# Two PSUM banks for the scores of the row maxima and two for the transposed scores and the turned maxima, instead of one pool of four

## The chip, the cores and the metric

The kernel runs on one core of a Trainium2 chip, and its time is device microseconds of one execution. The core has five engines that run side by side and meet through semaphores: TensorE (PE; its weight loads are listed apart, as PEld), VectorE (DVE), ScalarE (ACT), GpSimd (POOL) and SyncE (SP), which here issues transfers alone. PE writes its results into PSUM, which has eight banks of 128 partitions x 512 float32. PE works at a granted clock of 1.2 or 2.4 GHz, which the profile lists as 0.5 or 1.0.

## The reference

There are 8 batches of 8 heads, 576 positions and 64 columns. Each head is a causal attention with a decay bias that comes from running sums of `s`; the batch's rows, all heads side by side, then go through a selection of 128 of the 576 rows and a two-layer network for those rows alone.

```python
scores = scale * np.matmul(q, k.transpose(0, 1, 3, 2))
cum = np.cumsum(np.maximum(s, 0.0), axis=-1)
bias = -(cum[:, :, :, None] - cum[:, :, None, :])
scores = np.where(causal, -1000000000.0, scores + np.minimum(bias, 0.0))
scores = scores - np.max(scores, axis=-1, keepdims=True)
attn = np.exp(scores)
attn = attn / (np.sum(attn, axis=-1, keepdims=True) + 1e-09)
out = np.matmul(attn, v)
...
top_idx = np.argpartition(-(x @ w_gate)[b], capacity)[:capacity]
xe = x[b, top_idx]
ye = np.maximum(xe @ w1, 0.0) @ w2
out[b, top_idx] = xe + sigmoid(xe @ w_gate)[:, None] * ye
```

## The kernel before

**One head.** The 64 heads (8 batches x 8) are a stream through the same steps, and several heads are under way at a time. The scores of a head are computed twice. First with queries on the partitions, for the row maxima alone (`s_part`, line 335, in four parts): part 0 holds the query blocks 1 and 2 (192 and 320 columns), part 1 the blocks 3 and 0 (448 and 64), parts 2 and 3 the block 4 (512 and 64). Each part is one PSUM tile named `s`; DVE reads it with the mask and leaves the maximum (`s_max`, `mj<-s,maskf` in the profile; the result is `m`, of part 2 `md`). Then `m_rows` (line 372) has PE turn the 128 x 5 maxima into 5 x 128, ACT copies them out (`mr`), and a transfer lays them as a row into `qa`. With that row as one more line of the contraction, `st_part` (line 392) computes the transposed scores with their maxima subtracted, in higher precision by a second matmul into the same bank (`st<-qa,ka`, then `st<-qb,kb`); its parts 0 to 3 begin with 448, 320, 288 and 288 columns. ACT takes the exponential of each part (`pt<-st`), POOL clears the masked corner, and `av` multiplies by the values (`pa<-vt,pt`); DVE normalizes into `xt`.

**The batch's choice and network.** After a batch, `choose` scores the rows on DVE, turns the scores on PE in two tiles (`sct`, copied out by ACT as `row`), compares on DVE (`ahead`, `hit`), and sums positions on PE (`pidx`). `expert` does the network for two batches together, in small steps (`ph`, `py`) between the heads' steps. The last two batches' networks come after the last head.

**What sets the order.** Every engine runs its instructions in program order. A written list, `START`, gives the steps of the first heads, mixed with matmuls that only keep PE busy (`fill`, tile `warm`); after it a table, `SCHEDULE`, places each step of head n at slot 8n plus an offset. In the steady stretch PE's order in a head is: part 0 of `s` (head n+2), the last of `av`, part 1 of `s`, the turn of the maxima of head n+1, parts 0 and 1 of `st` (head n), three `av` products, part 2 of `s`, three more, part 3 of `s`, parts 2 and 3 of `st`, four more.

**The banks.** The pool `psS` (line 127) has four banks under one tag, `s`. Parts of `s`, parts of `st`, `sct` and `pidx` take whichever is free; the turned maxima are put into the last 128 columns of the bank of part 3 of `s` (kept as `st[n]["tp"]`, line 370), so that this bank is held until ACT has copied them out. After the last head, the tiles of the network take banks of this pool too (`bank`, line 589). `psA` has two banks for `pa`, `psM` two for the network, the warm matmuls and a few more.

Of the kernel before, what the change touches and what calls it, by code (L numbers as in the profile page):

```python
# [7 lines left out]
F32 = mybir.dt.float32  # L8
# [5 lines left out]
ALU = mybir.AluOpType  # L14
AX = mybir.AxisListType
PSUM = bass.MemoryType.PSUM
# [3 lines left out]
def _f(ap):  # L20
    return ap.bitcast(F32)
# [45 lines left out]
def kernel(  # L67
# [12 lines left out]
    pe, dve, act, pool, sp = (  # L80
        InOrder(tc, e) for e in (nc.tensor, nc.vector, nc.scalar, nc.gpsimd, nc.sync)
    )
    P = 128
# [4 lines left out]
    NT = (S + P - 1) // P  # L88
    LAST = S - (NT - 1) * P
    PAD = P - LAST  # L90
    SP = S + PAD
# [32 lines left out]
    small = ctx.enter_context(tc.tile_pool(name="small", bufs=3))  # L124
    moe = ctx.enter_context(tc.tile_pool(name="moe", bufs=1))
    dram = ctx.enter_context(tc.tile_pool(name="dram", bufs=2, space=bass.MemoryType.DRAM))
    psS = ctx.enter_context(tc.tile_pool(name="psS", bufs=4, space=PSUM))
    psA = ctx.enter_context(tc.tile_pool(name="psA", bufs=1, space=PSUM))
    psM = ctx.enter_context(tc.tile_pool(name="psM", bufs=2, space=PSUM))

# [149 lines left out]
    vts, xts, st = {}, {}, {}  # L280
# [46 lines left out]
    def s_max(n, u, scores, init=2.0 * NEG, c0=None, out=None):  # L327
        w = scores.shape[1]
        junk = small.tile([P, 512], BF16, tag="mj", name=f"mj{n}_{u}", bufs=2)
        dve.tensor_tensor_reduce(  # L330
            junk[:, 0:w], scores, maskf[:, S - w : S] if c0 is None else maskf[:, c0 : c0 + w], 1.0, init,
            ALU.add, ALU.max, out[:, 0:1] if out is not None else st[n]["m"][:, u : u + 1],
        )

    def s_part(n, part):
        i = n % NB
        ka, qa = KA[i], QA[i]
        if part == 0:
            st[n]["m"] = small.tile([P, NT], F32, tag="m", name=f"m{n}")
            st[n]["md"] = small.tile([P, 1], F32, tag="md", name=f"md{n}")  # L340
        R = RS
        tp = psS.tile([P, 512], F32, tag="s", name=f"s{n}_{part}")

        def mm(u, o_ap, c0):
            w = o_ap.shape[1]
            pe.matmul(
                o_ap, qa[0:R, u * P : (u + 1) * P], ka[0:R, c0 : c0 + w], start=True, stop=True
            )

        W = [LAST + u * P for u in range(NT)]  # L350
        if part == 0:
            a1, a2 = tp[:, 0 : W[1]], tp[:, W[1] : W[1] + W[2]]
            mm(1, a1, 0)
            mm(2, a2, 0)
            s_max(n, 1, a1)
            s_max(n, 2, a2)
        elif part == 1:
            a3, a0 = tp[:, 0 : W[3]], tp[:, W[3] : W[3] + W[0]]
            mm(3, a3, 0)
            mm(0, a0, 0)  # L360
            s_max(n, 3, a3)
            s_max(n, 0, a0)
        elif part == 2:
            mm(4, tp, 0)
            s_max(n, 4, tp, c0=0, out=st[n]["md"])
        else:
            a4 = tp[:, 0 : S - 512]
            mm(4, a4, 512)
            s_max(n, 4, a4, st[n]["md"][:, 0:1])
            st[n]["tp"] = tp  # L370

    def m_rows(n):

        i = n % NB
        m = st[n]["m"]
        row = QA[i][RM[i] : RM[i] + 1]
        tp = st[n]["tp"]
        if n == 0:
            tpm = psM.tile([P, 512], F32, tag="misc", name="tpm0")
            for t in range(NT):  # L380
                o_ap = tpm[0:1, t * P : (t + 1) * P] if t < 4 else tp[0:1, 512 - P : 512]
                pe.transpose(o_ap, m[:, t : t + 1], ident)
            act.activation(row[:, 0:512], tpm[0:1, :], AF.Copy, scale=-1.0)
            dve.tensor_scalar(row[:, 512:SP], tp[0:1, 512 - P : 512], -1.0, None, op0=ALU.mult)
            return
        tpm = tp[0:NT, 512 - P : 512]
        pe.transpose(tpm, m, ident)
        mr = small.tile([NT, P], F32R, tag="mr", name=f"mr{n}")
        act.activation(mr, tpm, AF.Copy, scale=-1.0)
        act.dma_start(_f(row).rearrange("a (t c) -> a t c", c=P), _f(mr))  # L390

    def st_part(n, part):
        i = n % NB
        R = RM[i] + 1
        ka, kb, qa, qb = ka_all[:, i, :], kb_all[:, i, :], QA[i], QB[i]
        if part == 0:
            st[n]["pt"] = ptp.tile([P, PTW], F32, tag="pt", name=f"pt{n}")
        pt = st[n]["pt"]
        tp = psS.tile([P, 512], F32, tag="s", name=f"st{n}_{part}")
        plan = [  # L400
            [(1, 0, cols[1])],
            [(2, 0, cols[2]), (3, 0, cols[3])],
            [(0, 0, HALF)],
            [(0, HALF, HALF), (4, 0, cols[4])],
        ][part]
        o = 0
        for t, c0, w in plan:
            kr = KR[t]
            ks = slice(t * P, t * P + kr)
            qs = slice(PAD + QB0[t] + c0, PAD + QB0[t] + c0 + w)  # L410
            pe.matmul(tp[0:kr, o : o + w], ka[0:R, ks], qa[0:R, qs], start=True, stop=False)
            pe.matmul(tp[0:kr, o : o + w], kb[:, ks], qb[:, qs], start=False, stop=True)
            o += w
        p0 = off[plan[0][0]] + plan[0][1]
        if part == 3:
            act.activation(pt[:, p0 : p0 + HALF], tp[:, 0:HALF], AF.Exp, scale=SCALE)
            act.activation(pt[0:R1, p0 + HALF : p0 + o], tp[0:R1, HALF:o], AF.Exp, scale=SCALE)
        else:
            act.activation(pt[:, p0 : p0 + o], tp[:, 0:o], AF.Exp, scale=SCALE)
        for t, c0, _ in plan:  # L420
            if c0 == 0:
                w = KR[t]
                pool.affine_select(
                    out=pt[0:w, off[t] : off[t] + w], in_=pt[0:w, off[t] : off[t] + w],
                    pattern=[[1, w]], compare_op=ALU.is_ge, fill=0.0, base=QB0[t] - t * P,
                    channel_multiplier=-1,
                )
# [158 lines left out]

    gs = {}

    def bank(shape, name):

        if finishing:
            return psS.tile(shape, F32, tag="s", name=name)
        return psM.tile(shape, F32, tag="misc", name=name)

    def expert(items):
# [5 lines left out]
        for j, (b, si, n, idx, xe) in enumerate(items):  # L601
            tpx = bank([P, NDT, P], f"xt{b}_{si}")
            for c in range(NDT):
                pe.transpose(tpx[:, c, 0:n], xe[0:n, c * P : (c + 1) * P], ident[0:n, 0:n])
            parts = [xh[:, :, P : 2 * P] if single else xl[:, :, j * P : (j + 1) * P]]
            parts.append(xh[:, :, j * P : (j + 1) * P])
            lo, hi = (x[:, :, 0:n] for x in parts)
            act.activation(hi, tpx[:, :, 0:n], AF.Copy)
            dve.tensor_tensor(lo, tpx[:, :, 0:n], _f(hi), op=ALU.subtract)
            if n < P:  # L610
                for x in parts:
                    dve.memset(_f(x[:, :, n:P]), 0.0)
            yield 1
            if not single:
                yield 1
# [3 lines left out]
        if single:  # L619
# [3 lines left out]
            def turn(f0):  # L623
                pt = bank([P, 4, P], name=f"pt{key}_{f0}")
                for f in range(f0, f0 + 4):
                    pe.transpose(pt[:, f - f0, :], hr[:, f * P : (f + 1) * P], ident)
                act.activation(hh[:, f0 : f0 + 4, 0:P], pt, AF.Copy)
                dve.tensor_tensor(
                    hl[:, f0 : f0 + 4, 0:P], pt, _f(hh[:, f0 : f0 + 4, 0:P]), op=ALU.subtract
                )  # L630

            turned = 0
            for f0 in range(0, F, 512):
                ph = bank([P, 512], name=f"ph{key}_{f0}")
                for a, (x0, wi) in enumerate(trip):
                    for c in range(NDT):
                        pe.matmul(
                            ph, xh[:, c, x0 : x0 + P], w1hl[:, wi, c, f0 : f0 + 512],
                            start=(a == 0 and c == 0), stop=(a == len(trip) - 1 and c == NDT - 1),
                        )  # L640
                    yield 1
                    if finishing and a == 0 and turned < f0 // P:
                        turn(turned)
                        turned += 4
                        yield 1
                act.activation(hr[:, f0 : f0 + 512], ph, AF.Relu)
# [85 lines left out]
    def run(op, n):  # L732
# [19 lines left out]
    AVU = [[0, 1], [2], [3], [4]]  # L752
    STAGES = dict(
        load=load, rows=rows, khi=khi, klo=klo, qhi=qhi, kb=kb, qb=qb, qlo=qlo, s=s_part, mrows=m_rows, st=st_part,
        av=lambda n, part: av(n, AVU[part]), norm=norm,
    )
# [10 lines left out]
    for slot_ in range(first, 8 * NH - 7 + max(pos for _, pos in SCHEDULE)):  # L767
        if slot_ >= 0 and slot_ % 2 and slot_ // 8 < len(CFG["fill"]):
            keep_warm(CFG["fill"][slot_ // 8])
        for op, pos in SCHEDULE:  # L770
# [3 lines left out]
            elif (slot_ - pos) % 8 == 0 and 0 <= (slot_ - pos) // 8 < NH:  # L774
                n = (slot_ - pos) // 8
# [57 lines left out]
```

## Time and profile before

| | |
|---|---|
| median of 3 runs | 522.47 us (521.87 to 522.79) |
| profiled execution, its own time | 521.27 us |
| its span (first to last instruction) | 519.6 us |
| PE busy / weight loads busy | 487.6 us / 447.5 us |
| DVE / ACT / POOL busy | 401.9 / 302.8 / 332.5 us |
| mean granted clock of PE | 0.982 |

A row of busy time counts an engine's instructions; of PE the ends are modelled, so that a short stop between two matmuls can hide in the row of the first. A row of waits names the engine that waited, the tile it was about to write and whose instruction ended the wait. A row of a timeline gives the start from the span's begin, the duration, the engine, the operation with its tiles and shapes, how many such instructions follow each other, and in brackets the engine's idle time before it and what ended that. L34 is the line of a helper that all instructions go through, so that the tiles' names tell the steps apart.

### The profile page before, as it was taken

To read this page: it belongs to the slowest core of one execution; us is meant where nothing else is said; L and a number is where in the kernel's file an instruction comes from. 1 tells how busy PE (TensorE), PEld (TensorE's weight loads), DVE (VectorE), ACT (ScalarE), POOL (GpSimd) and SP (SyncE) were. 2 spreads that over 40 slices of the span, in tenths; PEclk is the share of its full clock that TensorE was granted. 3 is DMA by queue.
4 is the path that set the end of the run, shared out by engine and by line. 5 is a ranking of instruction groups with operands and counts; after the bars stand their busy time and mean duration, and the time that the engine had idled before them with its cause. 6 is when DMAs were issued, how large, how long until landed. Compare 5 with 4: busy or idle time off the path is not lost.

```text
span 519.6 us, 11361 instructions
## 1 busy us (share of the span) xinstructions
PE 487.6 (94%) x3845; PEld 447.5 (86%) x3847; DVE 401.9 (77%) x1416; ACT 302.8 (58%) x658; POOL 332.5 (64%) x495
## 2 busy tenths in 40 slices
PE   6999998899988999899999999999999999999995
PEld 2688997889877889799999998999988898999774
DVE  7767898997689898977778986875689887763642
ACT  5566776667566767655555675654576665632121
POOL 6677777778678787865556774654778774523230
PEclk8899998999799999999999999999999999999999
DMA  4234542234324443322123332033242431011210
GB/s 165 79 103 117 183 142 75 89 100 142 105 78 154 135 119 114 118 93 80 41 93 120 113 119 73 2 119 112 73 141 65 143 107 40 8 46 42 67 40 21
DMA packets 23899, 49.08 MB, mean 94 GB/s; under 512 B 2537, under 2 KB 12068, under 8 KB 23842
## 3 DMA queue, kind: packets, MB, share of 16 engines
q1 hardware_dynamic: 19376, 39.52, 24.4%
q10 hardware_dynamic: 3186, 4.65, 2.9%
q0 software_dynamic: 1280, 4.20, 2.3%
q8 instruction: 30, 0.49, 0.4%
q14 instruction: 27, 0.22, 0.1%
HBM read 36.37 MB, written 11.53 MB: 92 GB/s over the span
## 4 chain that ended last, share of the span: by engine, by line
PE 58%; DVE 27%; issue 8%; DMA 3%; ACT 2%; POOL 1%; ACTq 0%; POOLq 0%; SPq 0%; DVEq 0%
PE pa L34 22%; PE st L34 14%; DVE mj L34 10%; PE s L34 7%; PE py L34 6%; DVE ahead L34 4%; DVE qb L34 3%; DVE junk L34 3%; PE warm L34 2%; DVE xt L34 1%; DMA out_dram<-xt 1%; DVE z L34 1%; ACT pt L34 1%; PE sct L34 1%; POOL hit L34 1%
## 5 line engine op out<-in xcount | busy, mean ns | idle before, releaser
L34 PE MATMUL pa<-vt,pt 128*96 128x95 f32 (+2 forms) x1920 | 227.4, 260 | 0.0
L34 PEld LDWEIGHTS pa<-vt,pt 128*96 128x96 f32 (+2 forms) x1920 | 214.7, 177 | 3.7 <-POOL pt L34 0.4
L34 ACT ACTIVATE pt<-st 128x288 f32<-128x288 f32 (+3 forms) x320 | 128.4, 439 | 105.2 <-PE st L34 88.5
L34 POOL TENSOR_SCALAR_AFFINE_SELECT pt<-pt 128x128 f32<-128x128 f32 (+1 forms) x320 | 108.1, 356 | 107.4 <-ACT pt L34 99.4
L34 DVE CUSTOM_DVE_ANT_0 mj<-s,maskf 128x192 bf16<-128x192 f32 (+4 forms) x320 | 139.8, 467 | 46.8 <-PE s L34 46.1
L34 PE MATMUL st<-qa,ka 67*128 67x288 f32 (+9 forms) x384 | 120.9, 326 | 19.1 <-DVE m L34 17.0
L34 PE MATMUL s<-ka,qa 66*128 66x64 f32 (+4 forms) x384 | 109.1, 342 | 3.6 <-DVE ka L34 3.6
L34 POOL TENSOR_TENSOR qb<-qk,qb 64x576 fp32r<-64x576 f32 x62 | 92.6, 1494 | 23.9 <-DVE qb L34 15.0
L34 PE MATMUL st<-qb,kb 128*128 128x288 f32 (+4 forms) x384 | 102.0, 302 | 0.0
L34 POOL TENSOR_TENSOR kb<-qk,ka 64x576 fp32r<-64x576 f32 x64 | 94.4, 1474 | 9.0 <-ACT ka L34 3.6
L34 PEld LDWEIGHTS st<-qa,ka 67*128 67x128 f32 (+3 forms) x384 | 71.9, 187 | 32.5 <-DVE m L34 27.1
L34 PEld LDWEIGHTS st<-qb,kb 128*128 128x128 f32 (+1 forms) x384 | 72.3, 188 | 0.8
L34 PEld LDWEIGHTS s<-ka,qa 66*128 66x128 f32 x384 | 65.5, 195 | 6.5 <-POOL kb L34 4.1
L34 ACT ACTIVATE kb<-qk 64x576 fp32r<-64x576 f32 x64 | 43.6, 682 | 5.5 <-DVE m L34 1.4
L34 ACT ACTIVATE qa<-qk 64x576 fp32r<-64x576 f32 x64 | 43.7, 683 | 4.9 <-DMA qa<-mr 1.5
L34 DVE CAST qb<-qk 64x576 fp32r<-64x576 f32 x64 | 44.8, 701 | 2.0
L34 ACT ACTIVATE ka<-qk 64x576 fp32r<-64x576 f32 x64 | 42.9, 670 | 3.7 <-DVE m L34 3.1
L34 DVE CUSTOM_DVE_ANT_0 junk<-xt,wg 128x512 bf16<-128x512 f32 (+1 forms) x40 | 34.9, 892 | 0.4
L34 ACT ACTIVATE mr<-s 5x128 fp32r<-5x128 f32 x63 | 16.5, 262 | 30.9 <-PE s L34 30.7
L34 DVE TENSOR_TENSOR xt<-pa,z 128x320 f32<-128x320 f32 x64 | 31.2, 487 | 0.1
L34 DVE SCALAR_TENSOR_TENSOR ahead<-row,sc,later 128x576 bf16<-128x576 f32 (+4 forms) x35 | 30.7, 878 | 0.6
L34 POOL DMA_INDIRECT out_dram<-xe,idx x8 | 8.8, 1104 | 33.5 <-DVE xe L34 23.5
(285 smaller groups left out, 536.6 us busy)
## 6 DMA issues: line engine op xcount, KB each, us to landing
qk<-in_qk_dram SPq DMA_DIRECT2D x31, 576.0 KB
vt<-in_v_dram SPq DMA_DIRECT2D x32, 325.0 KB
out_dram<-xt SPq DMA_DIRECT2D x16, 384.0 KB
wr<-in_w_dram ACTq DMA_DIRECT2D x16, 256.0 KB
out_dram<-xt SPq DMA_DIRECT2D x16, 192.0 KB
ka<-cumhl ACTq DMA_DIRECT2D x63, 4.5 KB
qa<-mr ACTq DMA_DIRECT2D x63, 2.5 KB
qk<-in_qk_dram SPq DMA_DIRECT2D x2, 288.0 KB
```

Of the source, the lines that this page charges most:

```text
L34: return self._tc.keep_in_program_order(call(*args, **kwargs))
```

## The change

The pool keeps four banks, now as two tags of two: `s` for the parts of the scores of the maxima (and for `sct` and `pidx`), `t` for the parts of the transposed scores and for the turned maxima, which get a tile of their own, `tpm`, at the turn. So the bank of part 3 of `s` is no longer held for the turn. After the last head the network's tiles take a bank of each tag by turns.

```diff
-    psS = ctx.enter_context(tc.tile_pool(name="psS", bufs=4, space=PSUM))
+    psS = ctx.enter_context(tc.tile_pool(name="psS", bufs=2, space=PSUM))
...
-            st[n]["tp"] = tp
...
-        tp = st[n]["tp"]
+
+        tp = psS.tile([P, 512], F32, tag="t", name=f"tpm{n}")
...
-                o_ap = tpm[0:1, t * P : (t + 1) * P] if t < 4 else tp[0:1, 512 - P : 512]
+                o_ap = tpm[0:1, t * P : (t + 1) * P] if t < 4 else tp[0:1, 0:P]
...
-        tpm = tp[0:NT, 512 - P : 512]
+        tpm = tp[0:NT, 0:P]
...
-        tp = psS.tile([P, 512], F32, tag="s", name=f"st{n}_{part}")
+        tp = psS.tile([P, 512], F32, tag="t", name=f"st{n}_{part}")
...
+    turns = [0]
+
     def bank(shape, name):
 
         if finishing:
-            return psS.tile(shape, F32, tag="s", name=name)
+            turns[0] += 1
+            return psS.tile(shape, F32, tag="st"[turns[0] % 2], name=name)
         return psM.tile(shape, F32, tag="misc", name=name)
```

The instructions of every engine stand in the same order as before; what moves is for whom an instruction waits. On PE in the steady stretch, before, from part 1 of `s` of head 18 (`s18_1`) over the turn of head 17 to the first two parts of `st` of head 16 (in brackets the semaphores that an instruction waits for, by the engine that raises them):

```order
L34 MATMUL s18_1_1726<-ka_89,qa_91 128x448 [waits Activation_49]
L34 MATMUL s18_1_1726<-ka_89,qa_91 128x64
L34 MATMUL s17_3_1683<-ident_116,m17_1626 5x128 [waits DVE_49]
L34 MATMUL st16_0_1739<-qa_91,ka_89 128x448 [waits DMAHW6_49,Activation_49]
L34 MATMUL st16_0_1739<-qb_92,kb_90 128x448
L34 MATMUL st16_1_1744<-qa_91,ka_89 128x320 [waits DVE_49]
```

The same place on PE with the change:

```order
L34 MATMUL s18_1_1743<-ka_89,qa_91 128x448 [waits DVE_49]
L34 MATMUL s18_1_1743<-ka_89,qa_91 128x64
L34 MATMUL tpm17_1750<-ident_116,m17_1642 5x128 [waits Activation_49]
L34 MATMUL st16_0_1757<-qa_91,ka_89 128x448 [waits DMAHW6_49,Activation_49]
L34 MATMUL st16_0_1757<-qb_92,kb_90 128x448
L34 MATMUL st16_1_1762<-qa_91,ka_89 128x320 [waits Activation_49]
```

Part 1 of `st` waited for DVE (in this head for the maxima of part 0 of `s` of head 18, whose bank it takes); it now waits for ACT, which copies the turned maxima out of the bank that it takes. Part 1 of `s` now waits for DVE's maximum of part 3 of the head before.

On PE in `START`, before, around the turn of head 0 and parts 2 and 3 of `s` of head 1:

```order
L34 MATMUL tpm0_230<-ident_116,m0_162 1x128 x3
L34 MATMUL s0_3_188<-ident_116,m0_162 1x128 [waits DVE_49]
L34 MATMUL s1_2_238<-ka_89,qa_91 128x512
L34 MATMUL s1_3_242<-ka_89,qa_91 128x64 [waits DVE_49]
L34 LDWEIGHTS warm_93
```

The same place on PE with the change:

```order
L34 MATMUL tpm0_231<-ident_116,m0_162 1x128 x3
L34 MATMUL tpm0_230<-ident_116,m0_162 1x128
L34 MATMUL s1_2_239<-ka_89,qa_91 128x512 [waits DVE_49]
L34 MATMUL s1_3_243<-ka_89,qa_91 128x64 [waits DVE_49]
L34 LDWEIGHTS warm_93
```

Part 2 took a free bank and now takes that of part 0 of the same head, after DVE's two maxima of it; part 3 took the bank of part 0 and now takes that of part 1, whose maxima DVE computes later.

Where a batch's choice falls between part 2 and part 3 of `s` (once a batch, here head 28), the tile `sct` takes one of the two `s` banks, and part 3 takes the bank of part 2. On PE with the change:

```order
L34 MATMUL s28_2_2720<-ka_89,qa_91 128x512 [waits DVE_49]
...
L34 MATMUL sct2_0_2730<-ident_116,sc2_2609 128x128 x2
L34 MATMUL s28_3_2735<-ka_89,qa_91 128x64 [waits DVE_49]
...
L34 MATMUL sct2_3_2795<-ident_116,sc2_2609 128x96 [waits DVE_49]
```

Before, part 3 there took a bank that ACT had read, and so did the second `sct`; now part 3 waits for DVE's maximum of part 2 just before it, and the second `sct` for DVE's maxima of part 0 of head 29.

## Rows read from the trace of the kernel before

**Rows 1.** The page's first part: busy us, share of the span, instructions.

```profile
PE 487.6 (94%) x3845; PEld 447.5 (86%) x3847; DVE 401.9 (77%) x1416; ACT 302.8 (58%) x658; POOL 332.5 (64%) x495
```

**Rows 2.** The waits of PE and of its weight loads, of two answers: who waited for whom, us in total, times, longest us.

```profile
PE st L34 <- DVE m L34: 17.0, 22, 1.7
...
PE st L34 <- DVE md L34: 1.2, 4, 0.5
...
PEld st L34 <- DVE m L34: 27.1, 27, 2.0
...
PEld st L34 <- DVE md L34: 2.9, 9, 0.7
```

**Rows 3.** Groups of instructions with shapes kept apart, PE: the first matmul of part 1 of `st`; busy us, mean ns, then idle before and what ended it.

```profile
L34 PE MATMUL st<-qa,ka 67*128 67x320 f32 x48 | 17.0, 355 | 14.3 <-DVE m L34 14.2
```

**Rows 4.** Windows, each from the first matmul of part 0 of `st` of one head to that of the next: length, then busy us of PE, PEld, DVE, ACT, POOL, the granted clock, the share of the DMA engines and GB/s.

```profile
101.60:108.31 6.71, 5.82 (x53) 5.39 (x51) 6.61 (x25) 4.30 (x9) 5.29 (x7) 1.00 0.63 180
120.88:126.39 5.51, 5.51 (x52) 5.42 (x51) 3.76 (x17) 4.18 (x9) 4.88 (x10) 1.00 0.04 13
132.20:142.81 10.61, 9.46 (x56) 8.96 (x55) 6.13 (x27) 4.79 (x10) 6.32 (x8) 0.68 0.23 70
378.26:385.55 7.29, 6.27 (x57) 5.83 (x56) 6.50 (x27) 4.68 (x10) 6.65 (x10) 1.00 0.19 74
```

**Rows 5.** Windows over several heads, the same columns.

```profile
95.40:115.40 20.00, 17.84 (x156) 16.46 (x154) 19.65 (x77) 12.81 (x27) 15.10 (x22) 1.00 0.26 78
...
148.70:171.60 22.90, 18.77 (x156) 16.67 (x154) 22.54 (x79) 14.06 (x30) 19.41 (x27) 1.00 0.36 111
...
202.00:217.10 15.10, 12.87 (x110) 11.67 (x108) 14.90 (x52) 10.23 (x22) 13.21 (x18) 1.00 0.34 102
...
285.10:292.30 7.20, 6.23 (x58) 5.71 (x55) 7.07 (x29) 4.29 (x9) 5.34 (x9) 1.00 0.10 37
...
391.10:411.00 19.90, 17.83 (x156) 16.43 (x154) 19.57 (x77) 12.79 (x27) 15.43 (x23) 1.00 0.25 78
```

**Rows 6.** Timeline of the head at 101.6: DVE's second maximum of part 0 of `s`, the first matmul of part 1 of `st`, and part 2 of `s`.

```profile
102.59 0.48 DVE L34 CUSTOM_DVE_ANT_0 mj<-s,maskf 128x320 bf16<-128x320 f32 x1
...
103.14 0.41 PE L34 MATMUL st<-qa,ka 67*128 67x320 f32 x1 [0.89 <-DVE m L34]
...
104.36 0.48 PE L34 MATMUL s<-ka,qa 66*128 66x512 f32 x1
```

**Rows 7.** Timelines around the turn of the maxima, of a head in which nothing waits (at 120.9: the turn, ACT's copy, the weight load and first matmul of part 1 of `st`) and of one in which ACT is late (at 73.9: the same matmul and copy).

```profile
120.85 0.27 PE L34 MATMUL s<-ident,m 128*5 128x128 f32 x1
...
121.16 0.27 ACT L34 ACTIVATE mr<-s 5x128 fp32r<-5x128 f32 x1 [0.40 <-PE s L34]
121.17 0.19 PEld L34 LDWEIGHTS st<-qa,ka 97*128 97x128 f32 x1
121.37 0.31 PE L34 MATMUL st<-qa,ka 97*128 97x320 f32 x1
...
74.44 0.31 PE L34 MATMUL st<-qa,ka 67*128 67x320 f32 x1
75.07 0.25 ACT L34 ACTIVATE mr<-s 5x128 fp32r<-5x128 f32 x1
```

**Rows 8.** Timelines where a batch's choice takes a bank (at 193: DVE's maximum of part 2 of `s`, then part 3; at 439.7: DVE's second maximum of part 0, then the second `sct`), and of part 1 of `s` at 131.6 with DVE's maximum of part 3 of the head before.

```profile
192.68 0.69 DVE L34 CUSTOM_DVE_ANT_0 mj<-s,maskf 128x512 bf16<-128x512 f32 x1
...
193.26 0.28 PE L34 MATMUL s<-ka,qa 66*128 66x64 f32 x1
...
439.72 0.49 DVE L34 CUSTOM_DVE_ANT_0 mj<-s,maskf 128x320 bf16<-128x320 f32 x1
439.73 0.33 PE L34 MATMUL sct<-ident,sc 96*128 96x96 f32 x2
...
131.58 0.48 PE L34 MATMUL s<-ka,qa 66*128 66x448 f32 x2
131.76 0.27 DVE L34 CUSTOM_DVE_ANT_0 mj<-s,maskf,md 128x64 bf16<-128x64 f32 x1
```

**Rows 9.** Timelines of `START`: DVE's second maximum of part 0 of head 0, then part 2 of head 0; part 2 and 3 of head 1 with DVE's last maximum of part 1 of that head; DVE's second maximum of part 0 of head 3 with parts 0 to 2 of head 3 (five matmuls).

```profile
11.15 0.49 DVE L34 CUSTOM_DVE_ANT_0 mj<-s,maskf 128x320 bf16<-128x320 f32 x1
11.21 1.04 PE L34 MATMUL s<-ka,qa 66*128 66x512 f32 x2
16.75 0.63 PE L34 MATMUL s<-ka,qa 66*128 66x512 f32 x2
18.10 0.22 DVE L34 CUSTOM_DVE_ANT_0 mj<-s,maskf 128x64 bf16<-128x64 f32 x1
27.40 1.05 PE L34 MATMUL s<-ka,qa 66*128 66x192 f32 x5
28.22 0.49 DVE L34 CUSTOM_DVE_ANT_0 mj<-s,maskf 128x320 bf16<-128x320 f32 x1
```

**Rows 10.** Windows around the stretches of low clock, columns as in Rows 4.

```profile
15.70:19.10 3.40, 3.40 (x21) 2.20 (x21) 2.72 (x11) 1.27 (x2) 1.43 (x2) 1.00 0.01 3
80.50:83.90 3.40, 1.74 (x14) 1.64 (x14) 3.37 (x15) 1.54 (x4) 3.01 (x5) 1.00 0.09 35
131.70:135.10 3.40, 2.20 (x16) 1.62 (x15) 3.30 (x18) 1.22 (x4) 2.63 (x4) 1.00 0.28 112
135.10:138.50 3.40, 3.40 (x17) 3.30 (x17) 1.95 (x8) 1.47 (x3) 2.23 (x3) 0.50 0.57 161
```

More of the change, by code (lines that the diff above doesn't have):

```diff
@@ L380, in m_rows @@
             for t in range(NT):
-                o_ap = tpm[0:1, t * P : (t + 1) * P] if t < 4 else tp[0:1, 512 - P : 512]
+                o_ap = tpm[0:1, t * P : (t + 1) * P] if t < 4 else tp[0:1, 0:P]
                 pe.transpose(o_ap, m[:, t : t + 1], ident)
             act.activation(row[:, 0:512], tpm[0:1, :], AF.Copy, scale=-1.0)
-            dve.tensor_scalar(row[:, 512:SP], tp[0:1, 512 - P : 512], -1.0, None, op0=ALU.mult)
+            dve.tensor_scalar(row[:, 512:SP], tp[0:1, 0:P], -1.0, None, op0=ALU.mult)
             return
-        tpm = tp[0:NT, 512 - P : 512]
+        tpm = tp[0:NT, 0:P]
         pe.transpose(tpm, m, ident)
```

## The prediction

> **What bounds the kernel now.** I read the page's busy times first: PE 487.6 of 519.6 us, DVE 401.9, ACT 302.8, POOL 332.5 [rows 1]. PE is nearly full, so time can come only from its stops, from loads that are not hidden, and from its clock. Then the waits of PE: the tiles `st` waited for DVE's maxima, 17.0 us in 22 waits and 1.2 us in 4; the weight loads waited 27.1 in 27 and 2.9 in 9 [rows 2]. By groups, 14.3 us of that stand before one matmul, the first of part 1 of `st` [rows 3]. A timeline shows why: DVE's maximum of 320 columns ends at 103.07, the matmul starts at 103.14 after 0.89 idle [rows 6]; it needed a bank whose reader had nothing to do with it. Last the windows of single heads: one with such a stop takes 6.71 us, one without 5.51 [rows 4]. The difference, 1.20, is 0.31 more than the idle shown (0.89), since the next weight load cannot run ahead of a stopped PE; I count 0.3 for each stop.
>
> **What is removed.** Idle 18.2 (17.0 + 1.2) in 26 waits, 26 x 0.3 = 7.8 for loads, and 10 waits that only loads show (36 - 26) x 0.3 = 3.0: 29.0 us gross. Not all of it pays. In five stretches, 85.1 us long in all, PE is busy 73.54 and DVE 83.73 [rows 5]: DVE is the engine that is full. PE idles 11.56 there, some 15 waits at the mean of 18.2 / 26 = 0.70; with 15 x 0.3 they hold 16.0 of the 29.0. What such a stretch can give is DVE's idle, 1.37, at the low end; at the high end one stop more at the edge of each, 5 x 1.20 + 1.4 = 7.4, if PE runs ahead before it and catches up behind it. I take 1.8, near the row of DVE's idle. Outside, 13.0 remain. In two heads with a choice (193 and its twin at 382) part 3 of `s` now takes the bank of part 2, whose maximum ends at 193.37, and the matmul stood at 193.26 [rows 8]: there the wait only moves, minus 2 x 1.20. So 10.6 + 1.8 = 12.4 us are gained.
>
> **What is added at part 1 of `st`.** It now takes the bank of the turned maxima, which ACT copies out. In a head where nothing waited the copy ends at 121.43 and the matmul started at 121.37, its load at 121.17 [rows 7]. With 0.05 for the release the matmul starts at 121.48, 0.11 later, and its load, hidden so far, shows for some 0.10: 0.22 a head. Behind the waiting matmul stand the rest of `st` and three products of `av`, all of PE's queue. 64 - 27 heads did not wait there for DVE [rows 2]; 13 of them have steps of the network or choice between the turn and this part, as I count them in the trace; 24 x 0.22 = 5.3. If all 37 paid it were 8.1, if only the 0.11 shows in 24, 2.6; I keep 5.3. In one head ACT is late, copy ending at 75.32 against a matmul at 74.44 [rows 7]: 0.9.
>
> **What is added at `s`.** In the steady stretch part 0 and part 2 of `s` now wait for DVE's maxima of each other, parts 1 and 3 for the others' of theirs. Part 2 starts at 104.36, the maximum it needs ended at 103.07 [rows 6]: over a microsecond of cover; the other parts have as much outside the full stretches. With a choice it is less. The second `sct` stood at 439.73, DVE's maximum ends at 440.21: 0.54, in two batches 1.1. One part 1 stood at 131.58, its maximum ends at 132.03 [rows 8]: 0.4 with some of it behind an earlier stop. Together 1.5. `sct` is read by ACT, with its row copies before all this, so nothing else is held. Behind the last head the network's tiles alternate between the tags; each product there is read by an engine soon after, and the last `exp` lies before them: about nothing, 0 to 0.5.
>
> **START.** Part 2 of head 0 started at 11.21 and must now wait for the maximum that ends at 11.64: 0.4 to 0.5. Part 2 and part 3 of head 1 stand at 16.75 to 17.38; part 3 takes the bank whose last reader ends at 18.32 [rows 9]; PE has nothing else there, 0.7 to 1.0. Parts 2 and 3 of `st` of head 0 come behind two exponentials, 0.4. Part 2 of head 3 starts with the fourth of five matmuls from 27.40 on (about 27.97) and the maximum ends at 28.71: 0.8. After fills that are hidden otherwise I add 3.0 (1.5 to 4).
>
> **Sum without the clock.** Costs 5.3 + 0.9 + 1.5 + 3.0 = 10.7, gain 12.4: minus 1.7.
>
> A sentence of the Trainium skill speaks against rings of two ("Perfetto Trace Analysis", section Optimizing Tensor Performance, Matmuls): independent groups of matmuls should rotate through different banks, so that the eviction of one overlaps the matmuls of the next. Rows 6 agree in that a bank's reader set PE's start, but the reader there was of another stream; by the rule fewer banks for each stream would cost, by the rows the coupling did.
>
> **The clock.** The granted clock falls behind a stop: in 131.7 to 135.1 PE is busy 2.20 of 3.4 us at 1.00, in 135.1 to 138.5 it is full at 0.50 [rows 10]. The head in which that happens takes 10.61 us at a mean of 0.68, the same kind of head at 378.26 takes 7.29 at 1.00 [rows 4]: 3.3. The stop of 80.5 to 83.9 (PE 1.74 of 3.4) has a like stretch behind it, mostly beside a full DVE (3.37 of 3.4) [rows 10]. I take it that the change shortens the wait ahead of the longer stretch enough that the clock stays up: minus 3.2. Against it, PE in START, full now from 15.7 to 19.1 [rows 10], gets about 1 us of idle.
>
> The skill's page "TensorE: Matmul & The Clock Gate" (section A second HAM failure mode: psum-queue depth-cycling) says that PE which stops briefly again and again while it cycles through few banks gets a clock that goes up and down; by it the short new stops at part 1 would cost clock in every head, which no row here shows, as all waits of rows 2 left the mean clock high.
>
> **Forecast.** 521.27 - 1.7 - 3.2 = 516.4 on the profiled execution's scale; the median lies 1.2 above it, so 517.5 us.
>
> **The rivals.**
> - The clock stays as it is, or its drop moves elsewhere, and the rest nets to minus 1.7 or a little less: 520.8. For it: the choice's heads have less slack after the change than before [rows 8]; against it: the waits ahead of the drop are among those removed.
> - Slower: two banks for `s` are too few. PE, no longer stopped at part 1 of `st`, stops at part 1 of `s` for DVE's last maximum of the head before, as the head at 131.6 would [rows 8]. Then the 10.6 outside the full stretches pay half, 5.3, and the full ones 1.4: 6.7 against 10.7, plus 4.0, with the low clock as before: 525.3, or 526.5 by the median. It decides once the freed waits pay under 9.7, a microsecond less than the costs. For it: DVE is full in 85 us [rows 5]. Against it: cover of over 1 us at part 2 [rows 6].
> - More: the full stretches give 7.4 in place of 1.8, and the turn's wait costs 0.11 in place of 0.22 in each of 24 heads, as its load may be issued before: 5.6 + 2.6 = 8.2 more, 508.2, by the median 509.4. For it: DVE's lead is used up at the heads between stretches; against it: DVE idles so little there.
> - The clock follows the new stops: START falls to 0.50 for a stretch (1.7 for 3.4 us) and the others stay: about 522.5 by the median, no change.
> - That it doesn't do what it says: the bank's wait goes by the names of the tiles; part 1 of `st` can then not wait for `m`. I give it nothing.
>
> **Chances.** Forecast 0.40 (514.5 to 519.5), first rival 0.22, slower 0.18, more 0.14, clock in START 0.06. Half of the first rival's and most of the last fall within 0.2% of the median (1.04 us), which is about what a measurement of this kernel tells from no change. Faster: 0.40 + 0.14 + 0.11 = 0.65; same 0.15; slower 0.20. The range reaches from inside the larger gain to the slower rival, 511 to 526; the likeliest case alone is 514.5 to 519.5.
>
> **What would show it.** Right: `st` no longer waits for DVE's `m` but for ACT's `mr`, by some 0.1 at a time; the stops left stand at `s` in the DVE-full stretches, and the sum of PE's idle falls by several microseconds; DVE's busy time is unchanged; the head at 132 runs at 1.00 in under 8 us. START is 2 to 4 us longer up to the first steady head. Wrong: many waits of `s` for DVE's `md` outside these stretches (the slower rival); waits for `mr` above 0.3; a clock that falls in a place where it did not fall before; stretches at 95 to 115 that get much shorter (DVE was not what bound them).

## The result

The changed kernel takes 529.49 us (median of 20 runs, 523.28 to 532.59) against 521.65 us of the kernel before (20 runs beside them, 517.04 to 528.29). The ratio is 1.0137, interval 1.0106 to 1.0167: it is slower by 1.4%. The ratio leaves out the two longest of these 20 runs, which stood apart as slow. Forecast was 517.5 us, range 511 to 526. The profiled execution took 530.31 us, its span 528.5 us, 8.9 more than before.

The page's first part of the changed kernel, which answers to [rows 1]:

```profile
PE 498.8 (94%) x3847; PEld 452.5 (86%) x3847; DVE 402.9 (76%) x1416; ACT 301.5 (57%) x658; POOL 330.1 (62%) x495
```

DVE, ACT and POOL have the work they had. PE is busy 11.2 us longer for the same instructions (3847 weight loads in both; two matmuls are missing from the row of before), so they took longer: that is either a lower clock or a wait that shows in the row of the matmul before it.

The windows of both kernels, cut at the same heads, show where the 8.9 us lie. First the kernel before (the length, then busy us of PE, PEld, DVE, ACT and POOL, then the granted clock):

```profile
0.00:38.19 38.19, 33.22 (x189) 22.91 (x191) 27.52 (x89) 22.08 (x40) 25.94 (x46) 0.91 0.36 118
...
79.90:89.40 9.50, 7.84 (x56) 7.41 (x55) 8.27 (x28) 5.78 (x13) 7.62 (x11) 0.82 0.08 31
89.40:132.20 42.80, 40.43 (x352) 38.18 (x350) 37.33 (x139) 29.79 (x64) 32.30 (x50) 1.00 0.39 118
132.20:142.80 10.60, 9.45 (x55) 8.95 (x55) 6.12 (x27) 4.79 (x10) 6.32 (x8) 0.68 0.23 70
...
171.60:177.40 5.80, 5.71 (x53) 5.51 (x50) 4.62 (x16) 4.33 (x10) 4.48 (x8) 1.00 0.71 223
...
209.00:217.10 8.10, 6.84 (x59) 6.26 (x58) 7.97 (x29) 5.00 (x11) 6.92 (x9) 1.00 0.59 182
217.10:519.60 302.50, 290.05 (x2304) 271.05 (x2301) 218.26 (x786) 157.24 (x352) 168.07 (x251) 1.00 0.24 76
```

The same stretches of the changed kernel:

```profile
0.00:41.17 41.17, 34.27 (x190) 22.61 (x191) 27.02 (x89) 22.64 (x40) 25.51 (x48) 0.92 0.32 109
...
82.60:94.20 11.60, 9.52 (x58) 8.57 (x56) 8.17 (x30) 5.23 (x12) 6.32 (x8) 0.71 0.01 4
94.20:137.00 42.80, 41.41 (x352) 38.12 (x349) 38.06 (x139) 29.53 (x64) 32.54 (x49) 1.00 0.39 119
137.00:144.30 7.30, 6.45 (x58) 5.83 (x55) 5.90 (x27) 4.68 (x10) 6.35 (x8) 1.00 0.29 97
...
173.10:183.00 9.90, 9.90 (x53) 9.56 (x51) 4.89 (x15) 4.82 (x10) 5.28 (x9) 0.53 0.39 124
...
215.00:224.70 9.70, 9.70 (x59) 9.18 (x57) 8.65 (x34) 4.82 (x11) 8.18 (x9) 0.65 0.45 144
224.70:528.50 303.80, 292.85 (x2304) 271.29 (x2302) 218.40 (x780) 156.73 (x352) 165.55 (x250) 1.00 0.24 75
```

`START` costs 3.0 us (41.17 against 38.19). The head at 132.2 lost its low clock, as forecast: 10.60 became 7.30. But the low stretch at 80 grew (9.50 to 11.60), and two heads that ran at 1.00 now run at 0.53 and 0.65 (5.80 to 9.90, 8.10 to 9.70). The long stretch of seven heads from 89.4 on, at 1.00 in both, takes 42.80 us in both: nothing was gained there. Read over the whole steady part, from the fourth head's first `st` to the last but one's, before and after:

```profile
38.19:465.87 427.68, 406.98 (x3376) 385.22 (x3374) 351.54 (x1258) 269.61 (x595) 292.79 (x430) 0.99 0.32 99
```

```profile
41.17:474.89 433.72, 417.17 (x3376) 390.51 (x3374) 353.05 (x1258) 267.78 (x595) 290.91 (x428) 0.97 0.31 98
```

So 3.0 us come from ahead of it, 6.0 from it; what follows takes 53.7 and 53.6 us.

The waits of PE and of its loads with the change (us in total, times, longest), which answer to [rows 2]:

```profile
PE s L34 <- DVE m L34: 7.8, 11, 1.3
PE s L34 <- DVE md L34: 4.6, 6, 0.9
...
PE pidx L34 <- DVE hit L34: 2.2, 5, 0.9
...
PE st L34 <- ACT mr L34: 1.0, 2, 0.8
PE sct L34 <- DVE m L34: 0.8, 2, 0.4
```

```profile
PEld st L34 <- ACT mr L34: 13.4, 37, 1.2
PEld s L34 <- DVE m L34: 12.6, 18, 1.5
PEld s L34 <- DVE md L34: 6.1, 6, 1.2
```

The waits of `st` for DVE, 18.2 us, are gone; 15.4 us stand at `s`, `sct` and `pidx` instead, for DVE as well, 1.4 of them in `START`. Before, no part of `s` waited for a maximum; the turn (its tile was called `s` too) did once, 0.7 us, and `pidx` once, 0.6. A wait of PE that is spread over 37 loads, for ACT's copy `mr`, is new.

Its timeline shows the copy, the load and the first matmul of part 1 of `st` in the head that answers to [rows 7]:

```profile
125.41 0.27 ACT L34 ACTIVATE mr<-tpm 5x128 fp32r<-5x128 f32 x1 [0.40 <-PE tpm L34]
...
125.72 0.19 PEld L34 LDWEIGHTS st<-qa,ka 97*128 97x128 f32 x1 [0.32 <-ACT mr L34]
125.72 0.42 PE L34 MATMUL st<-qa,ka 97*128 97x320 f32 x1
```

The load starts when the copy has ended, and the matmul at the same instant takes 0.42 in place of 0.31: the load is no longer hidden. No idle time of PE is printed, since the matmul before is taken to last until then; here such a wait is seen in PEld only. The head takes 5.73 us (125.12 to 130.85), where it took 5.51 without the wait [rows 4].

The granted clock falls to 0.50 three times: from 86.9 on, 1 us behind the start of part 2 of `s` of head 12, which had waited for DVE; from 172.2 on, behind two waits of the choice's `pidx`; from 216.1 on, behind part 1 of `s`:

```profile
85.94 0.50 PE L34 MATMUL s<-ka,qa 66*128 66x512 f32 x1 [1.32 <-DVE m L34]
...
169.94 0.18 PE L34 MATMUL pidx<-token,hit 128*128 128x1 f16 x1 [0.89 <-DVE hit L34]
170.76 0.40 PE L34 MATMUL pidx<-token,hit 96*128 96x1 f16 x2 [0.64 <-DVE hit L34]
...
214.60 0.50 PE L34 MATMUL s<-ka,qa 66*128 66x448 f32 x2 [1.29 <-DVE m L34]
```

Not every such stop brings the clock down: part 1 of `s` at 157.60 had waited 1.10 us for DVE, and from there to 161.0 the clock stays at 1.00.

In `START`, part 3 of `s` of head 1 waits as forecast:

```profile
18.44 0.30 PE L34 MATMUL s<-ka,qa 66*128 66x64 f32 x1 [0.79 <-DVE m L34]
```

### The profile page after: what moved, and what is told of

It is laid out like the page before. It is cut to its first block, busy times and chain, and to the rows that moved or that the text cites. A ratio compares the mean times of both kernels' runs of the same rounds, so it can differ in the third digit from the quotient of the medians.

```text
span 528.5 us, 11370 instructions
## 1 busy us (share of the span) xinstructions
PE 498.8 (94%) x3847; PEld 452.5 (86%) x3847; DVE 402.9 (76%) x1416; ACT 301.5 (57%) x658; POOL 330.1 (62%) x495
## 4 chain that ended last, share of the span: by engine, by line
PE 57%; DVE 28%; issue 8%; DMA 3%; POOL 2%; ACT 2%; POOLq 0%; SPq 0%; DVEq 0%; ACTq 0%
PE pa L34 21%; PE st L34 14%; DVE mj L34 10%; PE s L34 7%; PE py L34 6%; DVE ahead L34 4%; DVE junk L34 4%; DVE qb L34 3%; PE warm L34 2%; DVE xt L34 2%; DMA out_dram<-xt 1%; DVE z L34 1%; DVE hit L34 1%; PE tpm L34 1%; POOL hit L34 1%
## 5 line engine op out<-in xcount | busy, mean ns | idle before, releaser
L34 PE MATMUL pa<-vt,pt 128*96 128x95 f32 (+2 forms) x1920 | 230.7, 263 | 0.0
L34 PEld LDWEIGHTS pa<-vt,pt 128*96 128x96 f32 (+2 forms) x1920 | 218.2, 180 | 3.4
L34 ACT ACTIVATE pt<-st 128x288 f32<-128x288 f32 (+3 forms) x320 | 126.7, 438 | 104.1 <-PE st L34 96.3
L34 POOL TENSOR_SCALAR_AFFINE_SELECT pt<-pt 128x128 f32<-128x128 f32 (+1 forms) x320 | 105.8, 347 | 119.0 <-ACT pt L34 108.8
L34 PE MATMUL s<-ka,qa 66*128 66x64 f32 (+4 forms) x384 | 111.5, 347 | 17.5 <-DVE m L34 7.8
L34 PE MATMUL st<-qa,ka 67*128 67x288 f32 (+9 forms) x384 | 122.6, 330 | 1.5 <-ACT mr L34 1.0
L34 PEld LDWEIGHTS st<-qa,ka 67*128 67x128 f32 (+3 forms) x384 | 72.8, 189 | 15.8 <-ACT mr L34 13.4
L34 ACT ACTIVATE mr<-tpm 5x128 fp32r<-5x128 f32 x63 | 16.5, 262 | 42.6 <-PE tpm L34 42.5
L34 DVE CUSTOM_DVE_ANT_0 junk<-xt,wg 128x512 bf16<-128x512 f32 (+1 forms) x40 | 37.6, 961 | 0.4
```

The source lines that it names most:

```text
L34: return self._tc.keep_in_program_order(call(*args, **kwargs))
```

## The experiments

For each kernel the median is given, its ratio to the kernel before with the interval, and, as a measure of the clock, the mean over the runs that the ratio uses of time x (1 - mean granted clock): the us by which PE stood below full clock. It is 9.5 for the kernel before (71 runs beside the experiments) and 13.3 for the change (18 runs). It counts low clock beside other engines' work too, so it is more than what the clock costs.

**START alone.** The tiles of the first heads take a bank of either pair by a written table, as in

```diff
+        if name in FIRST:
+            kind = "sstt"[FIRST[name]]
+        return psS.tile([P, 512], F32, tag=kind, name=name)
```

> The change, but the tiles of the written list START take a bank of either pair, in the order in which they took the four before; after START the two pairs stay apart. Theory A (of the 8.9 us of span that the changed kernel is longer, about 3.0 come from START, whose first steady head begins at 41.2 in place of 38.2, the rest from stretches at the low clock): the fourth head begins at 38.2 to 38.6 and the time falls by about 3, to about 526.5 where the clock behaves as in the profiled run. Theory B (the split costs in the steady heads, START only shifts the rest): the later heads lose what START gains, and the time stays within 1 us of 529.5.

524.2 us, ratio 1.0073 (1.0038 to 1.0108). The fourth head begins at 37.91, and from the first matmul of `s` on the start takes 28.28 us against 31.53 of the change and 28.54 of before:

```profile
9.63:37.91 28.28, 28.06 (x179) 20.93 (x179) 20.62 (x80) 16.01 (x33) 18.65 (x30) 0.92 0.26 84
```

Theory A holds: START is worth 3 us. The median fell by 5.3; by the means of the compared runs (528.17 and 524.85) it is 3.3, of which the clock measure (12.3) has 1.0.

**The turn ahead of part 1 of `s`.** In `SCHEDULE`, `("mrows", -9)` moves from the end to just before `("s1", -17)`.

> The change, but on PE the turn of the maxima of head n+1 stands ahead of part 1 of s of head n+2 instead of behind it, so that ACT has 0.4 us more before part 1 of st wants the bank. Theory A (part 1 of st waits for ACT's copy in nearly every head outside the network's stretches, and a head takes 5.73 where one without wait took 5.51): these heads fall to about 5.5, the 37 waits of loads for mr vanish; some 20 such heads give 4 us: about 525.5 at an unchanged clock. Theory B (those heads are held by something else, the products' own pace or DVE): heads stay at 5.7 and the time at 529.5.

526.7 us, ratio 1.0082 (1.0042 to 1.0122), clock measure 13.0. A head that answers to the one of 5.72 us (119.40 to 125.12) of the change:

```profile
117.32:122.89 5.57, 5.57 (x52) 5.48 (x50) 3.72 (x17) 4.19 (x10) 4.01 (x6) 1.00 0.74 209
```

Theory A's mechanism holds: the head takes 5.57, and of the 37 waits of loads for `mr` 6 are left (1.7 us in place of 13.4). The 2.8 us by the median are less than the 4 expected. The clock does not account for that: its measure is about that of the change (13.3). But the turn, standing earlier, now waits for DVE's maxima itself:

```profile
PE tpm L34 <- DVE m L34: 6.4, 11, 1.3
```

With 2.9 and 5.4 us at `s` that makes 14.7 us of waits for maxima, where the change has 12.4 at `s` and none at the turn.

**The turned maxima in the network's pool.**

```diff
-        tp = psS.tile([P, 512], F32, tag="t", name=f"tpm{n}")
+        if n == 0:
+            tp = psS.tile([P, 512], F32, tag="t", name=f"tpm{n}")
+        else:
+            tp = psM.tile([P, 512], F32, tag="misc", name=f"tpm{n}")
```

> The change, but the turned maxima go into a bank of the network's pool and not into the pair of st. Theory A: no wait for mr, heads of 5.73 fall to about 5.5, so 4 us less (525.5 at an unchanged clock), a little given back where the network's tiles use the same two banks. Theory B: heads stay at 5.7; the network's stretches get longer and the time rises above 530.

522.57 us, ratio 0.9983 (0.9937 to 1.0028), 6.9 below the change. Windows over the heads 12 to 14 and of a single head:

```profile
95.29:114.98 19.69, 17.79 (x155) 16.90 (x154) 19.36 (x77) 12.53 (x27) 15.41 (x23) 1.00 0.25 79
114.98:120.51 5.53, 5.53 (x53) 5.44 (x51) 3.65 (x17) 4.19 (x9) 4.00 (x6) 1.00 0.70 214
```

The single head is back at 5.53 without the wait for ACT. The median fell by more than the 4 us of theory A; the clock measure is lower too (10.8 against 13.3). So two pairs of banks with the turn outside them cost nothing against the kernel before.

The heads 12 to 14, where DVE is busy 19.36 of 19.69, are as long as in the change (19.70) and nearly as before (20.00 [rows 5]). With the turn ahead they take less:

```profile
98.25:117.32 19.07, 17.80 (x154) 16.96 (x153) 18.74 (x77) 12.56 (x28) 15.30 (x22) 1.00 0.26 82
```

In all four DVE stands idle for 0.33 to 0.35 us of the three heads: their length is DVE's busy time, whichever wait of PE was moved. That time itself differs, since one comparison of the choice (`ahead`, 96 x 192) took 1.57 us before, 1.32 with the change and 0.95 with the turn ahead; why was not pursued.

**Both edits of the first two.**

> Both: START free as in e1 and the turn ahead as in e2. Theory A: the two gains add, 3 + 4 = 7 less than the change, about 522.5 at the changed kernel's clock of 0.970, and 516 if the clock is 0.982 as before. Theory B: within 1 us of the better of the two.

523.99 us, ratio 1.0078 (1.0042 to 1.0114), clock measure 13.6: above 522.5 and hardly better than START alone, with 29.0 us for the start and 5.57 for a single head. Less the clock measure, the means of the compared runs fall by 2.3 us with START free, 2.4 with the turn ahead and 4.4 with both: the two do add, each being smaller than expected, while the clock measure is 1.3 us above that of START alone. That pointed to the stops that are left.

**Filled stops.** Keep-busy matmuls (`warm`) go in front of the instructions at which PE stopped, so that PE works while it would wait; in the change 34 by a table and 6 ahead of one `pidx` (40 in all; the expectation says 43), in a third kernel, with START free and the turn in the network's pool, 54 (it says 49), in the kernel before 39.

```diff
     def run(op, n):
+        keep_warm(FILLS.get((op, n), 0))
```

> The change, with 43 matmuls that only keep PE busy (0.21 us each at full clock), put in front of the instructions at which PE stopped for 0.3 us or more in heads 9 to 29 of the profiled run, and about as long as each stop; nothing else differs. Theory A (of the 7 to 9 us, 4 to 6 are PE at the low clock behind such stops): the granted clock stays at 1.0 from 15 to 520 us, its mean rises from 0.974 to 0.985 or more, and the time falls by 4 to 6, to 523 to 525. Theory B (the low clock comes with the load or by itself, not from these stops; the fills only add work): the mean clock stays at 0.970 to 0.976 and the time is 529 to 533.

522.12 us, ratio 1.0016 (0.9994 to 1.0039), clock measure 4.4. No low clock is left between 17.5 and 519.3. The steady part of the filled change:

```profile
42.30:467.05 424.75, 415.83 (x3416) 383.57 (x3415) 351.99 (x1258) 267.42 (x595) 290.83 (x428) 1.00 0.32 100
```

It has 40 matmuls more than the change and takes 9.0 us less (433.72 - 424.75), at 1.00 in place of 0.97. Head by head, 52 of the 59 heads of this part take the same time in both, to 0.05 us. The three with the low clock of the change give the 9.0: the head at 82.58 falls from 11.58 to 9.19, that at 173.12 from 9.85 to 5.73, that at 214.97 from 9.76 to 7.28; the four others that differ cancel out. So it was the clock: theory A. The second of the three, with the fills:

```profile
171.20:176.93 5.73, 5.73 (x53) 5.35 (x51) 4.35 (x14) 4.31 (x10) 4.34 (x8) 1.00 0.70 213
```

> The kernel before, with 39 such matmuls in front of part 1 of st in eleven heads where PE stopped for DVE. Theory A: the kernel before also loses clock behind its stops, its loss falls from 9.6 to 5 to 7, the time to 517 to 519. Theory B: the time stays at 521.5 or rises by the fills.

516.57 us, ratio 0.9923 (0.9896 to 0.9949), clock measure 3.9.

```profile
38.10:462.69 424.59, 410.34 (x3414) 383.88 (x3413) 353.22 (x1257) 269.35 (x595) 293.21 (x430) 1.00 0.32 100
```

The kernel before gains 3.1 in the steady part (427.68 - 424.59), and the head at 132.20 alone gives 3.2 (10.61 to 7.42). With the clock up in both, the two kernels' steady parts differ by 0.2 us in these two executions; the one of the kernel before was 1.6 us above its median.

The third kernel, first without its fills:

> The change with START free as in e1 and the turned maxima in the network's pool as in e3. Theory A (START 3 us and the turn's wait are separate costs that add, the clock is a third): PE's work without the clock's part falls by 2.2 + 4.2 = 6.4 against the change, to about 508.5; with some 11 to 14 lost to the clock the time is 519.5 to 522. Theory B (what one frees the other takes): within 1 us of e3's 522.

521.9 us, ratio 0.9994 (0.9962 to 1.0025), clock measure 12.1; what remains without it is 508.3 (mean 520.3 - 12.1), as theory A said.

> f2 with 49 such keep-busy matmuls at the places where e3 stopped. Theory A: the clock's loss falls to 5 to 8 and the time to 514 to 517, below the kernel before (521.5). Theory B: no better than f2, 520 to 523.

514.1 us, ratio 0.9872 (0.9844 to 0.9901), clock measure 3.9: faster than both kernels of the case, and than the kernel before with fills. Its steady part:

```profile
38.36:459.10 420.74, 412.45 (x3429) 388.49 (x3428) 349.27 (x1258) 266.37 (x595) 292.69 (x427) 1.00 0.32 101
```

Against the filled change this is 4.0 less, the price of having the turned maxima in the pair of `st`, net of what else differs (START, and the tiles that now share the network's pool). Against the filled kernel before it is 3.9 less (2.5 by the medians of the two kernels): what two pairs of banks and the turn's move to the network's pool are worth together when the clock is held. The turn's move alone, with one pool of four, was not run.

**One place filled.**

> The change with keep-busy matmuls at two of the places only: five ahead of part 2 and three ahead of part 3 of s of head 12, around 84 to 88 us. Theory A (each low stretch hangs on the stops just ahead of it): no low clock at 80 to 95 us, the one near 170 stays; mean clock 0.978 to 0.982, time 525 to 527. Theory B (the clock is one budget for the whole run, or random): both stretches stay or both go; 529.5 or 522.

524.87 us, ratio 1.0085 (1.0055 to 1.0115), clock measure 10.4.

```profile
82.50:91.70 9.20, 8.43 (x63) 6.63 (x63) 8.15 (x29) 5.30 (x12) 6.06 (x8) 1.00 0.04 13
...
155.30:165.60 10.30, 10.30 (x50) 9.94 (x51) 7.45 (x31) 4.82 (x10) 7.50 (x9) 0.50 0.45 144
```

The stretch behind the filled place stays at 1.00, and 11.60 us become 9.20. The other low stretch stays but comes 17 us earlier than in the change, behind another stop while DVE works at the same batch's choice: part 1 of `s` at 155.14, which waited 1.09 us for DVE. It is the stop that stood at 157.60 in the change (1.10 us) and left the clock alone there. So theory A holds for the place that was filled; at which of several stops that are left the clock falls was not settled. That fills elsewhere than at the stops would do nothing was not tried.

**A lighter DVE.**

> The change with less work for DVE: the maximum of part 2 of s reads 64 of its 512 columns (0.22 in place of 0.69 us a head, by the shapes of the page), and the exponentials have their argument divided by 1024 so that they stay finite; so the maxima of the last query block and the exponentials' values are left out, every instruction stays. Theory A (in the DVE-full heads DVE sets the pace, and the waits of PE at s are its lateness): heads 12 to 14, 19.7 us together in the change, fall by 3 x 0.47 to 18.3, PE's waits at s for DVE fall from 12.4 us to under 7, and heads that had only the wait for the turn's copy stay at 5.73. Theory B (the ring of two banks itself holds PE): heads 12 to 14 stay above 19.3.

> The kernel before with the same lighter DVE (maximum of part 2 of 64 columns, exponentials' argument divided by 1024). Theory A: heads 12 to 14, 20.0 us together, fall to about 18.6, and the waits of st for m from 17.0 us to under 9: those waits were DVE's lateness, not the shared banks' doing. Theory B (the shared banks made them): the waits for m stay above 12 us.

516.77 us with the change (4 runs), ratio 0.9904 (0.9866 to 0.9943), and 509.28 us without (2 runs), ratio 0.9776 (0.9742 to 0.9810). The heads 12 to 14, of the lighter change and then of the lighter kernel before:

```profile
95.75:114.62 18.87, 18.21 (x156) 16.59 (x154) 18.55 (x77) 12.57 (x27) 15.25 (x23) 1.00 0.26 83
```

```profile
93.07:111.51 18.44, 17.61 (x156) 16.32 (x154) 18.10 (x75) 12.60 (x27) 14.93 (x23) 1.00 0.28 85
```

Without the change these heads fell by 1.56, about the 1.41 that was taken off DVE (3 x 0.47); with it by 0.83, which lies between the two theories. But DVE's busy time there fell by as much, 1.55 (19.65 to 18.10) and 0.82 (19.37 to 18.55), since DVE's other instructions took longer in sum in the lighter change, and DVE idles 0.34 and 0.32 us as in the runs above: DVE sets the pace there in both.

The waits, of the lighter change and then of the lighter kernel before:

```profile
PE s L34 <- DVE m L34: 4.4, 8, 1.1
...
PE s L34 <- DVE md L34: 2.7, 6, 0.6
```

```profile
PE st L34 <- DVE m L34: 14.3, 21, 1.7
```

That the waits at `s` fell from 12.4 to 7.1 us fits DVE as their source, just above the 7 that was named. In the lighter kernel before, the waits of `st` for `m` are still 14.3 us, where theory A wanted less than 9: it failed in this. Whether the shared banks make these waits or a DVE that is still nearly full (18.10 of 18.44) was not separated.

**The own tile alone.**

> One part of the change alone: the kernel before with its one pool of four, where the turned maxima have a bank of their own at the turn instead of part 3's. By the order of the banks part 1 of st still takes the bank of part 0 of s in 53 of 64 heads. Theory A (the split does it, not the own tile): the waits of st for m stay at 15 to 19 us, no wait for mr, 520.5 to 523. Theory B (the own tile, as a ninth user of the four banks, costs): 525 or more.

522.4 us, ratio 1.0030 (1.0003 to 1.0057).

```profile
PE st L34 <- DVE m L34: 15.9, 21, 1.5
```

A bank for the turn costs little in one pool of four, and the waits for `m` stay: it is the split that takes them away from `st`. Nor do two pairs make the time longer by themselves: with the turn in the network's pool the ratio is 0.9983.

## Why the prediction was wrong

Two steps failed: the clock, which was counted as 3.2 us won and became a loss, and the new waits at `s`, put at 1.5 us outside two heads, which took most of the gain of 12.4.

**The clock (failed).** The prediction counted 3.2 us as won for the low stretch at 132. The rivals let the drop stay, move elsewhere or take START; none let it grow. The stretch did go, and was worth what was said: 10.60 to 7.30. There was some luck in it: with the turn in the network's pool, part 3 of `s` of the same head waited 1.20 us in place of 0.85, the clock fell behind it, and the head took 9.17. And the same argument works the other way too: waits that are moved can bring the clock down where they go, and some went to places where PE had not stopped for long, so that it fell where it did not fall before. The prediction had named that as a sign of being wrong, but gave it no cost beyond the old one. Two of `pidx` make 1.53 us of stops within the 3.4 us before 172.2:

```profile
168.80:172.20 3.40, 1.75 (x18) 1.44 (x17) 3.31 (x11) 1.42 (x4) 2.41 (x4) 1.00 0.46 107
```

It is the picture of [rows 10], PE 1.74 of 3.4 and then a clock of 0.50, at a new place. The picture alone does not settle it: in the 3.4 us before 157.60 PE is busy 1.68 and the clock stays. The filled kernels put a number on the term: in the profiled executions low clock costs the steady part 9.0 us with the change and 3.1 without, so in place of -3.2 it was +5.9. Over all runs it is less. The clock differs from run to run, from 0.966 to 0.982 in the 20 of the change, and the profiled one had 0.970 where the median is 0.975; by the medians the fills gave 7.4 us with the change and 4.6 without, so +2.8.

**The waits at `s` and the gain (failed).** 12.4 us less the 1.5 at `s`, so 10.9, were expected. With the clock held the split gave 3.9 (424.59 to 420.74), 2.5 by the medians, and that with the turn out of the way. That DVE fills five stretches was right, and the yield there small: 20.00 to 19.70 in heads 12 to 14. The error lies outside them. 13.0 us, less 2.4 for two heads, were counted there, as if behind a freed wait PE went on without another, with a cover of over a microsecond at `s`. Instead it met DVE a little later: outside START the parts of `s` wait 11.0 us for maxima. In the head at 378.26, which is at 386.75 in the change, the wait went from part 1 of `st` to part 3 of `s`, and the head takes 7.34 in place of 7.29 [rows 4]; that was foreseen for two such heads and holds for six, by the six waits for `md`. The working has 15 waits in the full stretches where 11.56 / 0.70 is 16.5; that moves the gain by half a microsecond only.

**The turn's wait (right).** 0.22 a head was expected, 5.3 us, and 0.9 in one late head, 6.2 together; measured 0.22 in the head shown (5.73 against 5.51) and 4.0 in all. The loads that wait number 37 where 24 were counted; the price in all was lower all the same, since in the DVE-full heads the wait costs nothing: heads 12 to 14 take 19.71 us in the filled change and 19.69 in the third kernel.

**START (right).** 3.0 expected, 3.0 measured in the profiled executions (31.53 against 28.54 from the first matmul of `s` on). The stop ahead of part 3 of head 1, forecast as 0.7 to 1.0, is 0.79.

**The sum.** In the profiled executions 3.0 + 5.9 + 0.2 = 9.1 against 8.9 of the span, and the clock is two thirds of the loss. By the medians the loss is 7.8 us (529.49 - 521.65) and the clock 2.8 of it, about a third; the filled kernels stand 5.5 apart (522.12 and 516.57), which leaves some 2.5 for the steady part beside the 3.0 of START. So START and the clock are each shown to cost, and how the loss divides is known only within these bounds. The slower rival had the right side and half of the mechanism: PE does stop at part 1 of `s` for DVE, and the freed waits pay no more than the steady costs. But it left the low clock as before.

The profiled executions of the filled kernels stand 4.3 apart, of which the first part is 4.2 (42.30 against 38.10). About 1 us of this is the clock again: in the filled change PE is still at 0.50 from 16 to 17 us, where the change itself is at 1.00.

The short stops for `mr`, one a head, did the clock no harm: the seven heads from 94.2 on run at 1.00. It fell behind the stops of 1.3 us and of 0.9 and 0.6 shown above. The Trainium skill ("TensorE: Matmul & The Clock Gate", section A second HAM failure mode: psum-queue depth-cycling) tells of a kernel that cycles through PSUM banks and whose PE stops briefly between groups of matmuls so often that its clock goes up and down. The trace agrees for some of the longer stops and not for the short ones.

## What to carry to other kernels

A freed wait is worth nothing until the next thing that this engine waits for has been named, and here that was the same engine, DVE, a few instructions later. When waits of PE are moved, look for the places where they gather, since behind stops of about a microsecond the clock can fall (here to 0.50, for some 6 to 10 us at a time) and cost several more; matmuls that only keep PE busy, put exactly where it would wait anyway, gave 7.4 us in the change and 4.6 before, by the medians. A change of banks is best read in three parts, the start, the steady part and the clock, since each can hide the others.

## What was not expected

Saving waits did not lower the clock's loss: with START free and the turn ahead together the clock measure is 13.6, with START alone 12.3, and the medians are 0.2 us apart. The lighter kernel before had no low clock between 16.1 and 507.6 us though it kept 14.3 us of waits for `m`, the longest 1.7; how much PE waits in all does not tell whether its clock falls.
